# Banded attention and gated MLP on one core: folded score edges, a shared bank for the half middles, engine orders from a table, and a weight load in five pieces

## The chip, the cores and the metric

The kernel runs on one core of a Trainium2 chip (trn2). The metric is device time in microseconds (us) of one execution; lower is better. The core has five engines that each run their own instructions in order: PE (TensorE, matmuls), ACT (ScalarE), DVE (VectorE), POOL (GpSimd) and SP (SyncE, which here only issues DMAs). They wait for each other through semaphores.

## The reference

```python
mod = (_silu(c) @ w_mod).reshape(1, 6, 1, -1)          # sa, ca, ga, sb, cb, gb
h = _layernorm(x) * (1 + ca) + sa
x = x + ga * A(h, wqkv, wo)        # 16 heads of 28, S = 2048, D = 448
h = _layernorm(x) * (1 + cb) + sb
x = x + gb * B(h, w_in, w_sp, b_sp, w_out)

# A: causal attention in a window of 256 keys
mask = (i - j >= 0) & (i - j < 256)
p = softmax(where(mask, q @ k.T * Dh ** -0.5, -1e9));  o = (p @ v) @ wo
# B: gated MLP, Fh = 896
z = gelu(x @ w_in);  z1 = z[..., :Fh];  z2 = layernorm(z[..., Fh:])
g = w_sp @ z2 + b_sp               # w_sp is 2048 x 2048, over the tokens
out = (z1 * g) @ w_out
```

All tensors are bfloat16; the batch is 1.

## The kernel before

The 2048 tokens are 16 tiles of 128 (index j or t) and four blocks of 512 (tb). The 16 heads are four groups of four heads; a head takes 32 partitions, so that a group fills 128.

**Start.** Two x loads of two tiles each (`t_x0`, L427), `w_mod` (`t_wmA`) and the query and key weights (`t_wq`) are loaded on the DMA queues of SP and of ACT. DVE takes layernorm statistics of tiles 0 to 3 (L603), POOL the reciprocal root (L608, L609), DVE normalises (L616), PE transposes (L682) and ACT or DVE scale and shift into `hT` (L691, L693). `t_wqk` (L595, L596) casts the weights into `WQK`. PE then makes queries and keys (L760, L785) and values (L798).

**Attention.** A tile of queries needs key blocks j-2 (the old edge), j-1 (the middle, all 128 x 128) and j (the new edge, causal). It is worked in two halves of two head groups. For each half the score block (L901) writes four PSUM banks (0 to 3, one for each head of a group) with 36 small matmuls of 32 contraction rows: the middle of the first group (128 columns) and, for both groups, the old and the new edge folded together by 64 queries and keys into 192 columns. The middle of the second group comes from one matmul (L910) with `QBD`, a block-diagonal copy of the queries that four small DMAs fill from `qT` (L751, L777); it takes a fifth bank. ACT exponentiates (L862) 2048 columns of the four banks and 512 of the fifth, into a buffer of `PW`. DVE multiplies the folded edges by the mask into `PT` (L917, two for each half), and PE multiplies with the values (L944). DVE normalises the result into `o_sb` (L958, L960), a DMA transposes it, PE multiplies by `wo` (L969), DVE adds to x (L973), and the second layernorm follows (L603, L608, L609, L620, L616 or L622, a padding copy L625 or L626, a DMA transpose, L992 or L994).

**MLP.** PE multiplies by `w_in` in tiles of 64 rows: z2 (L1066) and z1 (L1087). ACT applies gelu (L1073, L1095), DVE normalises z2 (L603, L1078). SP issues 32 DMA transposes of `w_sp` into `wspA` and `wspB`, whose memory is that of `QBD`, `qT`, `KT` and `PT`, so that most of them wait for the end of attention. PE multiplies z2 by them (L1110, 28 groups of 16 matmuls), DVE adds `b_sp` (L1114), POOL multiplies by z1 (L1117), PE multiplies by `w_out` (L1127, 16 tiles), DVE adds x (L1137), and SP stores.

**Order.** Every operation is recorded with the engines it may run on, its dependences, a priority and a guessed duration. Before the program is written, `Sched.order` plays a greedy planner over these guesses: it fixes the order on every engine, the engine of each operation recorded by `either` or `free`, and the PSUM bank or buffer (`Hold`) each takes. `count` and `waits` then place semaphores. DMA landings of the first loads are given as fixed times (`land`). On the engines nothing is reordered.

Of the kernel before, what the change touches and what calls it, by code (L numbers as in the profile page):

```python
# [9 lines left out]
HOP = 0.12  # L10

BIAS = 0.0

NEXT = {"dve": 0.08, "act": 0.11, "pool": 0.045}

SHAPE = 0.1

TURN = 1.1
# [11 lines left out]
class Res:  # L30
# [6 lines left out]

    def best(self):
        found = None
        for o in self.options:  # L40
            at = 0.0
            for u in o:
                h = self.last[u]
                if h is None:
                    continue
                if not h.until or any(x.end is None for x in h.until):
                    at = None
                    break
                at = max([at] + [x.end for x in h.until])
            if at is not None and (found is None or at < found[0]):  # L50
                found = (at, o)
        return found
# [35 lines left out]
class Sched:  # L88
# [23 lines left out]
    def order(self):  # L112
        ready = {e: [] for e in ENGS}
        for op in self.ops:
            op.left = len(op.deps)
            for d in op.deps:
                d.users.append(op)
        free = {e: 0.0 for e in ENGS}
        table = [None]
        turned = [True]  # L120
        shape = ["full"]
        self.prog = {e: [] for e in ENGS}
        dma_at = [0.0]

        def enter(op):
            op.ready = max([0.0] + [d.start + d.ways["pe"][0] if d.eng == "pe" and "pe" in op.ways else d.end for d in op.deps])
            for e in op.ways:
                ready[e].append(op)

        for op in self.ops:  # L130
            if not op.left:
                enter(op)
        todo = len(self.ops)
        while todo:
            pick = None
            for e in ENGS:
                found = []
                for op in ready[e]:
                    if any(x.start is None for x in op.after):
                        continue  # L140
                    at = max(op.ready, free[e])
                    ok = True
                    for h in op.take:
                        b = h.res.best()
                        if b is None:
                            ok = False
                            break
                        at = max(at, b[0])
                    if ok:
                        found.append((at + (BIAS if e == "act" and len(op.ways) > 1 else 0.0), op))  # L150
                if not found:
                    continue
                first = max(free[e], min(a for a, _ in found))
                at, op = min(((a, o) for a, o in found if a <= first + 1e-9), key=lambda x: (x[1].prio, x[1].n))
                if pick is None or at < pick[0]:
                    pick = (at, e, op)
            assert pick is not None, "no op can go on"
            at, e, op = pick
            if e == "act" and len(op.ways) > 1:
                at -= BIAS  # L160
            for h in op.take:
                _, slot = h.res.best()
                h.slot = slot
                for u in slot:
# [5 lines left out]
            dur, fns = op.ways[e]  # L170
            if e == "act" and op.table and op.table != table[0]:
                dur += 1.3
            if e == "pe" and op.shape != shape[0]:
                dur += SHAPE
                shape[0] = op.shape
            if e == "sp":
                if op.turn and not turned[0]:
                    dur += TURN
                turned[0] = op.turn
            op.eng, op.start = e, at  # L180
            free[e] = at + dur - NEXT.get(e, 0.0)
            if op.land is not None:
                op.end = max(at + 1.0, op.land)
                dma_at[0] = max(dma_at[0], op.end - 2.0)
            elif op.dma:
                dma_at[0] = max(dma_at[0], at + 1.0) + op.lat
                op.end = dma_at[0] + op.tail
            else:
                op.end = at + dur + HOP + op.lat
            if e == "act" and op.table:  # L190
                table[0] = op.table
            for x in op.ways:
                ready[x].remove(op)
            self.prog[e].append(op)
            todo -= 1
            for u in op.users:
                u.left -= 1
                if not u.left:
                    enter(u)
# [1010 lines left out]
```

## Time and profile before

| | |
|---|---|
| timed runs | 289.79, 290.8, 291.15 us; median 290.8 |
| span of the profiled execution, first to last instruction | 288.0 us (the page gives no other time for it) |
| PE busy | 274.4 us (95%), 3432 matmuls |
| DVE, ACT, POOL busy | 170.3, 131.8, 123.4 us |
| DMA | 25.92 MB |
| granted PE clock | 1.00 throughout |

The page describes one execution; its durations are used against its own span of 288.0 us, which lies 2.8 us under the median of the timed runs. Differences worked out on the span are added to the median. "Busy" for PE counts pipelined matmuls to their modelled ends, so that two matmuls overlap in it: the distance from one start to the next says more of what a matmul costs than its duration does. A line of the form "A <- B: 5.6, 14, 0.5" says that A waited 5.6 us in total for B, 14 times, 0.5 us at most.

### The profile page before, as it was taken

To read this page: it belongs to the slowest core of one execution; us is meant where nothing else is said; L and a number is where in the kernel's file an instruction comes from. 1 tells how busy PE (TensorE), PEld (TensorE's weight loads), DVE (VectorE), ACT (ScalarE), POOL (GpSimd) and SP (SyncE) were. 2 spreads that over 40 slices of the span, in tenths; PEclk is the share of its full clock that TensorE was granted. 3 is DMA by queue.
4 is the path that set the end of the run, shared out by engine and by line. 5 is a ranking of instruction groups with operands and counts; after the bars stand their busy time and mean duration, and the time that the engine had idled before them with its cause. 6 is when DMAs were issued, how large, how long until landed. Compare 5 with 4: busy or idle time off the path is not lost.

```text
span 288.0 us, 7864 instructions
## 1 busy us (share of the span) xinstructions
PE 274.4 (95%) x3432; PEld 151.4 (53%) x3432; DVE 170.3 (59%) x365; ACT 131.8 (46%) x153; POOL 123.4 (43%) x192
## 2 busy tenths in 40 slices
PE   6798889999999999999979999999999999999997
PEld 2595557567666765544445544444444444444443
DVE  7679996988889999879998101113211231123223
ACT  4487979999999988775656720000000000000000
POOL 8041690761470749898654113333133303330331
DMA  7845936244233685320199899940100010001001
GB/s 213 267 156 148 326 60 95 54 83 92 39 41 76 112 166 58 60 58 18 39 186 167 194 175 190 186 77 17 49 0 0 2 64 0 2 0 64 0 2 64
DMA packets 65349, 25.92 MB, mean 90 GB/s; under 512 B 56417, under 2 KB 64226, under 8 KB 65314
## 3 DMA queue, kind: packets, MB, share of 16 engines
q1 hardware_dynamic: 64496, 24.26, 40.3%
q10 hardware_dynamic: 818, 1.15, 1.3%
q8 instruction: 27, 0.44, 0.7%
q14 instruction: 8, 0.07, 0.1%
HBM read 9.01 MB, written 1.84 MB: 38 GB/s over the span
## 4 chain that ended last, share of the span: by engine, by line
PE 64%; DVE 20%; POOL 5%; DMA 5%; issue 2%; SPq 2%; ACT 1%; ACTq 1%; POOLq 0%
PE ps L1110 34%; PE ps L1127 7%; PE ps L1087 5%; DVE st_all L603 5%; DVE PT L917 5%; PE ps L785 4%; DMA wq_st<-in_A_wqkv_dram 3%; PE ps L944 2%; POOL rs_all L609 2%; PE ps L798 2%; PE ps L1066 2%; PE ps L901 2%; PE ps L725 2%; DVE xn L616 1%; DVE x_sb L973 1%
## 5 line engine op out<-in xcount | busy, mean ns | idle before, releaser
L862 ACT ACTIVATE PW<-ps 128x2048 bf16<-128x2048 f32 (+1 forms) x56 | 69.4, 1239 | 4.5 <-PE ps L901 3.2
L1117 POOL TENSOR_TENSOR z1T<-tmpg,z1T 128x512 bf16<-128x512 bf16 x28 | 32.3, 1153 | 89.9 <-DVE tmpg L1114 89.9
L1114 DVE TENSOR_TENSOR tmpg<-ps,bsp_bc 128x512 bf16<-128x512 f32 x28 | 19.4, 692 | 85.3 <-PE ps L1110 85.3
L1110 PE MATMUL ps<-wspB,z 128*128 128x512 bf16 x224 | 48.8, 379 | 0.0
L1110 PE MATMUL ps<-wspA,z 128*128 128x512 bf16 x224 | 48.7, 379 | 0.0
L917 DVE TENSOR_TENSOR PT<-PW,mask 128x1024 bf16<-128x1024 bf16 x56 | 38.7, 718 | 0.7 <-ACT PW L862 0.3
L1110 PEld LDWEIGHTS ps<-wspA,z 128*128 128x128 bf16 x224 | 21.9, 98 | 26.5 <-issue 0.4
L1110 PEld LDWEIGHTS ps<-wspB,z 128*128 128x128 bf16 x224 | 21.9, 98 | 26.4
L608 POOL TENSOR_SCALAR ve_all<-mv_all 128x1 f32<-128x1 f32 (+2 forms) x37 | 10.1, 274 | 47.3 <-DVE mv_all L606 46.5
L944 PE MATMUL ps<-Vaug,PT 128*128 128x32 bf16 x496 | 26.2, 177 | 2.8 <-issue 1.7
L944 PEld LDWEIGHTS ps<-Vaug,PT 128*128 128x128 bf16 x496 | 22.9, 96 | 7.0 <-issue 1.8
L609 POOL TENSOR_TENSOR rs_all<-ve_all,neghalf 128x1 f32<-128x1 f32 (+2 forms) x37 | 24.8, 672 | 2.0
L1066 PE MATMUL ps<-w_in,hT 64*128 64x448 bf16 x224 | 22.4, 349 | 2.1 <-POOL rs_all L609 1.7
L1087 PE MATMUL ps<-hT,w_in 64*128 64x512 bf16 x196 | 21.8, 376 | 0.0
L1127 PE MATMUL ps<-w_out_g,z1T 128*128 128x448 bf16 x112 | 21.8, 352 | 0.0
L944 PE MATMUL ps<-Vaug,PW 128*128 128x32 bf16 x224 | 21.7, 176 | 0.0
L944 PEld LDWEIGHTS ps<-Vaug,PW 128*128 128x128 bf16 x224 | 17.9, 96 | 2.9
L603 DVE BATCH_NORM_STATS2 st_all<-x_sb 128x6 f32<-128x448 bf16 x32 | 18.9, 609 | 0.4 <-DMA x_sb<-in_A_x_dram 0.3
L1073 ACT ACTIVATE z<-ps 128x896 bf16<-128x896 f32 x16 | 13.9, 915 | 11.2 <-PE ps L1066 11.2
L603 DVE BATCH_NORM_STATS2 st_all<-z 128x6 f32<-128x448 bf16 x32 | 18.1, 594 | 1.0 <-ACT z L1073 1.0
L622 POOL TENSOR_SCALAR xn<-x_sb,rs_all,ve_all 128x448 bf16<-128x448 bf16 x17 | 18.1, 1066 | 0.9
L1066 PEld LDWEIGHTS ps<-w_in,hT 64*128 64x128 bf16 x224 | 11.0, 94 | 12.5 <-ACT z1T L1095 2.1
(106 smaller groups left out, 370.1 us busy)
## 6 DMA issues: line engine op xcount, KB each, us to landing
out_dram<-fin SPq DMA_DIRECT2D x16, 112.0 KB, 1.7
x_sb<-in_A_x_dram SPq DMA_DIRECT2D x3, 448.0 KB, 4.4
wmod<-in_w_mod_dram SPq DMA_DIRECT2D x1, 1344.0 KB, 8.0
w_in<-in_B_w_in_dram SPq DMA_DIRECT2D x1, 1344.0 KB, 8.2
w_out_g<-in_B_w_out_dram SPq DMA_DIRECT2D x1, 784.0 KB, 5.4
QBD<-qT SPq DMA_DIRECT2D x12, 64.0 KB, 2.0
bsp_bc<-in_B_b_sp_dram SPq DMA_DIRECT2D x1, 512.0 KB, 5.4
wmod<-in_w_mod_dram SPq DMA_DIRECT2D x2, 224.0 KB, 6.2
```

Of the source, the lines that this page charges most:

```text
L603: st = [dve(0.62 if True else 0, lambda e, t=t, ci=ci, s=s: e.bn_stats(st_all[:, slot, t, ci, :], s()), deps(t), prio) for ci, s in enumer ...
L609: rs = pool(0.53 + 0.15 * len(tiles), lambda e: e.tensor_tensor(rs_all[:, slot, a:b], ve_all[:, slot, a:b], neghalf[:, 0:b - a], ALU.pow), ...
L622: "pool": (0.9, lambda e: e.tensor_scalar(to[:, h.slot[0], 0:D], x_sb[:, t, :], z, ve, ALU.mult, ALU.add))}, [nm], prio, [h])
L862: ex = act(xdur, lambda e, out_ap=out_ap, in_ap=in_ap: e.activation(out_ap(), in_ap(), ACT.Exp, scale=SCALE), [s], v - 8.0 + u, takes, tab ...
L917: return dve(0.70, lambda e: e.tensor_tensor(cols(hp.slot[0] * 2048 + 1024 * k, [[256, 4], [128, 2], [1, 128]]), cols(at_w() + 128 + 192 * ...
L944: fns.append(lambda e, hp=hp, hO=hO, hi=hi, bi=bi, kb=kb, hd=hd, nb=nb, a=at[hi][bi], p_of=p_of: e.matmul(ps[:, hO.slot[0], 32 * hd:32 * h ...
L1066: return lambda e, kc, p0, start, stop: e.matmul(ps[:, hs[t % 2].slot[hf], 0:D], lhsT=hT[p0:p0 + 64, kc, t * 128:(t + 1) * 128], rhs=w_in[ ...
L1087: return lambda e, kc, p0, start, stop: e.matmul(ps[:, hs[b // 2].slot[b % 2], :], lhsT=w_in[p0:p0 + 64, kc, ft * 128:(ft + 1) * 128], rhs ...
L1110: m = pe(16 * MMS, [lambda e, h=h, si=si, ft=ft, tb=tb: e.matmul(ps[:, h.slot[0], :], lhsT=z2[:, si, ft * 128:(ft + 1) * 128], rhs=(wspA i ...
L1114: a = dve(0.7, lambda e, h=h, ht=ht, tb=tb: e.tensor_tensor(tmpg[:, ht.slot[0], :], ps[:, h.slot[0], :], bsp_bc[:, tb * 512:(tb + 1) * 512 ...
L1117: u = pool(1.16, lambda e, ht=ht, ft=ft, tb=tb: e.tensor_tensor(z1T[tb][:, ft, :], tmpg[:, ht.slot[0], :], z1T[tb][:, ft, :], ALU.mult), [ ...
L1127: return [lambda e, ft=ft: e.matmul(ps[:, h.slot[0], 0:D], lhsT=z1T[t // 4][:, ft, (t % 4) * 128:(t % 4 + 1) * 128], rhs=w_out_g[:, ft, :] ...
```

## The change

- **Edges folded by 32.** The old edge is computed for all 128 queries and the new edge written over its masked parts in pieces of 32 keys: 160 columns a group instead of 192, in 48 matmuls a half instead of 36. The mask reads `PW` with a step of 32 instead of 64.
- **Half middles.** The room gained in each bank (64 columns) takes 64 queries of the second group's middle. The other 64 queries of both halves come from two `QBD` matmuls of 256 columns into one bank, with one exponential of 512 columns for a tile instead of two. `QBD` is half as large, with runs of 128 elements in its DMAs (before 512 or 256), and zeroed by two instructions instead of four. `QP` reorders the groups in `qT`. `PW` has three buffers of a tile instead of five of a half.
- **Table.** The planner is replaced by `PLAN`: 1127 words, each an engine, an operation's number and its buffer choices. Some loads of the start change place: ACT's queue issues c, w_mod, the activation table load, w_q, and then the second x load, which was first. The 28 w_sp groups stand in another order, ahead of all `w_out` tiles.
- **w_in** is loaded in five pieces, each after a score block of tiles 4 to 8; before, three DMAs right after the x loads.
- Some guessed durations, landings and pacing dependences change.

```diff
+PLAN = """
+a0 d25 t32 s8 d27 t31 d26 a3 t33 s1 t35 t36 t34 d50 t37 p55.0 d24 s7 d23 p60.1 a42 d90 s5 t30 p57.2 d28 d91 s4
...
+p1018.4 d1117.3 s1122 s1118 p1123.7 d1019.2 s1020 p1124 d1125.1 s1126 p52.3
+"""
...
     def order(self):
-        ready = {e: [] for e in ENGS}
...
+        names = {"p": "pe", "a": "act", "d": "dve", "t": "pool", "s": "sp"}
         self.prog = {e: [] for e in ENGS}
...
+        for at, word in enumerate(PLAN.split()):
+            n, *slots = map(int, word[1:].split("."))
+            op = self.ops[n]
+            for h, k in zip(op.take, slots):
+                h.slot = h.res.options[k]
+                for u in h.slot:
                     old = h.res.last[u]
                     if old is not None:
                         op.deps.update(old.until)
                     h.res.last[u] = h
             op.deps.discard(op)
...
+            op.eng = names[word[0]]
+            assert op.eng in op.ways
+            op.end = at
+            self.prog[op.eng].append(op)
...
-    NPW = 5
+    NPW = 3
+    QP = (2, 0, 3, 1)
+    PWT = 576
+    PWH = 4 * PWT
...
-    QBD, _, qbd_bytes = alloc("QBD", [128, 2, 2, 4, 512], BF16, at=wspA_off)
+    QBD, _, qbd_bytes = alloc("QBD", [128, 2, 4, 2, 256], BF16, at=wspA_off)
...
-                 land=(3.0, 3.3)[i]) for i in range(2)]
+                 land=(3.65, 3.9)[i]) for i in range(2)]
...
-    t_win_l = load2("d_win", "sp", 1.4, w_in, ALL, B_w_in, ALL, prio=-46.0)
-
-    t_win_l.append(load("d_winc", "sp", 0.25, lambda e: e.dma_start(w_in[64:128, 3, :], B_w_in[384:448, :]), (), -45.9))
-    late += t_wo + t_win_l
+    late += t_wo
+    t_win_l = [load("d_win%d" % ch, "sp", 0.46, lambda e, ch=ch: e.dma_start(w_in[:, ch, :], B_w_in[ch * 128:(ch + 1) * 128, :]), (), -46.0 + 0.1 * ch)
+               for ch in range(3)]
+    t_win_l += [load("d_winh%d" % p0, "sp", 0.23, lambda e, p0=p0: e.dma_start(w_in[p0:p0 + 64, 3, :], B_w_in[384:448, :]), (), -45.6 + 0.001 * p0)
+                for p0 in (0, 64)]
...
-    PACE = {1: 0, 2: 18, 3: 34}
-    PSTEP = 1.0
+    PACE = {1: 0, 2: 15, 3: 27}
+    PSTEP = 0.75
...
-                        QBD[32 * hh:32 * hh + 32, tb % 2, :, hh, :],
-                        qT[32 * hh:32 * hh + 32, tb % 2].rearrange("p (a b) n -> p a b n", b=2)[:, :, 1, :]))},
+                        QBD[32 * hh:32 * hh + 32, tb % 2, hh].rearrange("p a (m n) -> p (a m) n", m=2),
+                        qT[32 * hh:32 * hh + 32, tb % 2, 0:2].rearrange("p a (m n) -> p (a m) n", m=2)[:, :, 64:192]))},
...
-                for place in (((0, m, 128, 0, 128, 0, 0),), ((k, o, 128, 0, 64, 128, 0) for k in range(2)), ((k, n, 128, 64, 128, 256, 0) for k in range(2)),
-                              ((k, *e) for k in range(2) for e in ((n, 64, 0, 64, 192, 0), (o + 64, 64, 64, 128, 192, 64)))):
...
+                places = [(0, m, 128, 0, 128, at_m0, 0)]
+                places += [(k, o, 128, 0, 128, at_f[k], 0) for k in range(2)]
+                places += [(1, m, 128, here, here + 64, at_hm, 0)]
+                places += [(k, n, 128, 96, 128, at_f[k] + 128, 0) for k in range(2)]
+                places += [(k, n + 32 * g, 32, 32 * g, 96, at_f[k] + 32 * (g + 1), 32 * g) for k in range(2) for g in range(3)]
...
-                unit(EPRI, MMS, [lambda e, hC=hC, m=m, half=half, qi=qs[1], j=j: e.matmul(
-                    ps[:, hC.slot[0], :].rearrange("p (h q) -> p h q", h=4), lhsT=KT[:, qi, m:m + 128],
-                    rhs=QBD[:, (j // 4) % 2, half, :, (j % 4) * 128:(j % 4 + 1) * 128], start=True, stop=True)],
-                     need + [q_dma[j // 4]], 0.6, to_e, lambda hC=hC: ps[:, hC.slot[0], :], [], hC)
...
+                    exC = unit(EPRI, 0.22, [lambda e, hC=hC, m=m, hh=hh, j=j, pair=pair: e.matmul(
+                        ps[:, hC.slot[0], 256 * hh:256 * hh + 256].rearrange("p (h q) -> p h q", h=4), lhsT=KT[:, 2 * hh + 1, m:m + 128],
+                        rhs=QBD[:, (j // 4) % 2, :, hh, pair:pair + 64], start=True, stop=True) for hh in range(2)],
+                         needC + [q_dma[j // 4]], 0.6, to_c, lambda hC=hC: ps[:, hC.slot[0], :].rearrange("p (a h q) -> p a h q", a=2, h=4), [], hC)
...
+    for n, d in enumerate(t_win_l):
+        d.deps.add(S_of[WIN_AT[n]][0])
```

More of the change, by code (lines that the diff above doesn't have):

```diff
@@ L36, in __init__ @@
         self.last = {u: None for u in units}
[L38 to L52, printed above, removed]
 class View(Res):
@@ L112, in order @@
     def order(self):
-        ready = {e: [] for e in ENGS}
[L114 to L121, printed above, removed]
-        self.prog = {e: [] for e in ENGS}
[L123 to L164, printed above, removed]
@@ L169, in order @@
             op.deps.discard(op)
[L170 to L199, printed above, removed]
+            op.eng = names[word[0]]
+            assert op.eng in op.ways
+            op.end = at
+            self.prog[op.eng].append(op)
+        assert sum(map(len, self.prog.values())) == len(self.ops)
     def count(self):
@@ L411, in load2 @@
         ]
-    t_c = load("d_c", "act", 0.01, lambda e: e.dma_start(c_row[:], c[0:1, :]), prio=-98.97, land=3.7)
+    t_c = load("d_c", "act", 0.01, lambda e: e.dma_start(c_row[:], c[0:1, :]), prio=-98.97, land=4.0)
     def x_load(e, i):
@@ L861, in unit @@
                 S_of[j].append(s)
-                ex = act(xdur, lambda e, out_ap=out_ap, in_ap=in_ap: e.activation(out_ap(), in_ap(), ACT.Exp, scale=SCALE), [s], v - 8.0 + u, takes, table="exp")
+                ex = act(xdur, lambda e, out_ap=out_ap, in_ap=in_ap: e.activation(out_ap(), in_ap(), ACT.Exp, scale=SCALE), [s] + list(after), v - 8.0 + u, takes, table="exp")
                 if exs:
```

144 lines of the change are left out of this document (103 added, 41 removed).

## The prediction

> **What bounds the kernel now.** I read the windows first, cut where the work changes: the first score block of tile 2 (30.1), the last product with the values (121.9), the first w_sp group (167.05), the last `w_out` matmul (285.1). Columns: stretch, length, then busy PE, PE weight loads, DVE, ACT, POOL with instructions.
>
> ```profile
> core 0: us, PE busy (x) PEld busy (x) DVE busy (x) ACT busy (x) POOL busy (x), PEclk, DMA share, GB/s
> 18.45:30.10 11.65, 10.10 (x175) 7.04 (x173) 9.69 (x24) 9.49 (x11) 4.12 (x8) 1.00 0.46 138
> 30.10:121.90 91.80, 87.81 (x2117) 58.02 (x2119) 83.56 (x171) 82.61 (x82) 53.78 (x82) 1.00 0.50 92
> 121.90:167.05 45.15, 43.01 (x415) 21.72 (x413) 34.51 (x85) 28.29 (x44) 26.37 (x55) 1.00 0.60 115
> 167.05:285.10 118.05, 118.05 (x563) 54.89 (x562) 28.52 (x43) 1.52 (x4) 32.30 (x28) 1.00 0.24 48
> ```
>
> After 167.05 PE never stops: only an earlier start of that stretch shortens the kernel. From 30.1 to 121.9 three engines are about 90% busy. Next the waits, which tell who holds whom there, and the groups with one shape a row.
>
> ```profile
> PEld ps L901 <- ACT PW L862: 5.6, 14, 0.5
> PE ps L901 <- ACT PW L862: 0.7, 2, 0.4
> ACT PW L862 <- PE ps L901: 3.2, 8, 0.6
> PE ps L910 <- DMA QBD<-qT: 1.1, 2, 0.7
> ```
>
> ```profile
> L862 ACT ACTIVATE PW<-ps 128x2048 bf16<-128x2048 f32 x28 | 52.7, 1881 | 3.7 <-PE ps L901 3.2
> L862 ACT ACTIVATE PW<-ps 128x512 bf16<-128x512 f32 x28 | 16.7, 598 | 0.8
> L917 DVE TENSOR_TENSOR PT<-PW,mask 128x1024 bf16<-128x1024 bf16 x56 | 38.7, 718 | 0.7 <-ACT PW L862 0.3
> ```
>
> The score block waits for its four banks, which the exponential of the half before still reads. Last the timeline, which gives distances between starts, the loads of the start and the w_sp transposes:
>
> ```profile
> 1.29 0.61 ACTq L413 DMA_DIRECT2D c_row<-in_c_dram  x1
> 1.93 0.40 ACTq L421 DMA_DIRECT2D wmod<-in_w_mod_dram  x1
> 2.36 0.49 ACTq L421 DMA_DIRECT2D wq_st<-in_A_wqkv_dram  x1
> 3.66 1.15 DVE L603 BATCH_NORM_STATS2 st_all<-x_sb 128x6 f32<-128x448 bf16 x2 [0.31 <-DMA x_sb<-in_A_x_dram]
> 12.99 1.06 PE L760 MATMUL ps<-hT,WQK 128*128 128x128 bf16 x16
> 142.63 20.20 SPq L479 DMA_TRANSPOSE wspA<-in_B_w_sp_dram  x14
> 167.05 3.19 PE L1110 MATMUL ps<-wspA,z 128*128 128x512 bf16 x14
> ```
>
> PE work from 30.1 to 121.9, by start distances: 28 score blocks 0.48 each, 27 `QBD` matmuls 0.22, 60 value products (12 matmuls in 0.295), 12 key blocks 0.895, 13 values and 14 `wo` tiles 0.765, 12 query blocks 0.86, 7 warming pairs 0.43, 1.5 of L1066: 83.0. So the 91.8 are 83.0 of work and 8.8 of waiting.
>
> **The change, part by part.**
>
> *Score block.* In one block of before, 4 matmuls of 128 columns take 0.05, 16 of 64 columns 0.10, then PE pauses about 0.1, 16 pieces of 64 keys run in 0.06 and it pauses 0.1 again: matmuls of different row groups run side by side, so columns count and not instructions. The new block has 0.05 + 0.107 (8 of 128) + 0.027 (4 of 64) + 0.027 (8 of 32), a pause, 24 pieces in two waves of 96 columns (0.08), a pause: 0.48 + 0.07 = 0.55. Bounds: 0.48 (all hidden in the pauses) and 48/36 x 0.48 = 0.64 (a fixed cost for each). x28: +2.0 (0 to +4.5).
>
> *Shared bank.* A `QBD` pair of 256 columns costs 0.22 once a tile, not twice: -3.1 of PE. ACT loses 14 x 0.598 = 8.4. The 2048-column exponential and the mask keep their sizes (steps of 576 and 32 elements instead of 512 and 64): nothing, bounds -/+0.03 on 56 masks. Zeroing `QBD` loses two instructions of 1.05 on ACT before 15 us, ahead of x: nothing.
>
> *What the table gives each engine,* from the order of instructions. ACT, first to last exponential: the 8.4, plus three key copies (0.597), two value copies (0.544), one query copy: -4.9 of 92. DVE, from the first `hT` to the last `o_sb`: three value copies, two key copies, three scalings (0.49), statistics of one tile less, two normalisations (0.503) and three paddings (0.309) more: -3.7. POOL -3.4, off the path.
>
> *Start.* The second x load is now last on ACT's queue. Before, that queue landed in order: x at 3.9 (224 KB), w_mod at 8.2 (448 KB more), w_q at 10.1 (448 more). The same bytes before it put x at about 10.1. DVE runs in order: its statistics of tiles 2 and 3 stand ahead of the casts of `WQK` and the copies to `modT`, and PE's first queries wait for these. 10.1 + two statistics 1.07 + aggregate 0.1 + two xn 0.7 + aggregate 0.15 + POOL's add and power 1.47 (6.21 to 7.68 before) + two xn 0.7 + two casts 0.69 + `hT` 0.4 + hops 0.3 = 15.6, against 12.99: +2.6 (low end +0.7, if it lands with w_mod at 8.2). The first exponential goes with it, 20.46 to 23.0. ACT has the last query copy behind that, so it ends at 24.6 (before 21.2, on DVE). The `QBD` DMAs on SP wait for it, behind them the x loads of blocks 2 and 3 (+3.4); PE's first `QBD` matmul waits for the DMAs: 25.6 + 3.4 = 29.0. The table puts it ahead of tile 2's score block: 29.2, where before it was 30.1. The late start is thus not lost twice, but paid in work moved behind: half of tile 1's scores, two values, one key block.
>
> *Attention.* PE's work behind 29.2 is 83.0 - 3.1 + 2.0 + 3.2 (moved) = 85.1. The waits: a half of a tile has 0.175 less of ACT (4.9/28) and 0.13 less of DVE (3.7/28); 0.15 x 28 = 4.2 off PE's 8.8, most of which were for exponentials. Bounds: 0 (the order ties PE elsewhere) and 6.8 (2 us left). Waits 4.6.
>
> *w_in.* SP waits for PE (tiles 4 to 8) before each piece, and block 1's fourth `QBD` copy stands behind the first, as do four transposes of xn. A 448 KB load took 4.4 to land, so that copy lands some 5.4 after the score block of tile 4; the `QBD` matmul is due 4.6 after it: up to 0.8, I take +0.4. The DMAs of 26 to 36 us get room, worth nothing, as x did not wait for them after 28.2.
>
> The `QBD` copies move half the bytes in runs of 256 B (before 1 KB). Landing took 2.0 for 64 KB in 1 KB runs and 2.1 for 32 KB in 512 B runs: a fixed time, so nothing. [...]
>
> *Tail.* From the last `o_sb` (122.4) to the first w_sp group were 44.7. PE has 42.0 of work there; the table puts 22 us of it, not 11, ahead of what needs block 2, which ends the wait of 1.7 at 145.9. But the last `hT` transpose came 18.9 after that `o_sb`, behind it 14 transposes of w_sp at 1.44, the last landing 3.8 after its issue: 42.9. Now it is 15 (one of `wspB` has slipped in) and DVE has 0.3 more ahead: 44.5. So 44.7 stays. `b_sp` is loaded after 29 transposes instead of before `wspB`: about 69.9 after the last `o_sb`; the ninth group needs a free bank at 72.3. Hidden, with 2.4 to spare; what is later than that PE waits. Group and `w_out` order: 28 x 3.45 + 16 x 1.33, as before.
>
> Sum: 29.2 + 85.1 + 4.6 + 0.4 = 119.3 against 121.9: -2.6, so a span of 285.4, and 290.8 - 2.6 = **288.2**.
>
> **Rivals.**
> *Waits that grow (slower).* The table was fixed for guessed times, with the second x load at 3.9; an order that meets another timing makes each engine stand before the wrong instruction. In PE's attention, waits a third over 8.8 (11.7) give 29.2 + 85.1 + 11.7 + 0.4 = 126.4, +4.5: 295.3; waits of 8.7 already give +1.5, the point from which it is slower. For it: three engines at 90%, and DVE blocked on x to 10.1. Against: ACT and DVE are lighter.
> *w_sp takes the gain (no difference).* If DVE's z2 statistics, five of which stand ahead of the last tiles' additions, push the last `hT` transpose 2 later, the groups start 2 later whatever attention gained: 290.2.
> *x lands early or order gains more.* Queues that interleave would land x near 5; or the order leaves 2 of waiting. Either is worth 2.6 more: 285.6. Against: the queue's order at 3.9, 8.2, 10.1.
> That the table does not do what it says is excluded by the listed order.
>
> **How the numbers follow.** Runs of this kernel tell apart about 0.5% (1.45 us): the three lie within 1.36. Forecast 0.42, x early or better order 0.15, both faster: 0.57. w_sp: 0.18, within 0.5%. Waits that grow: 0.25. The range goes from 282.5 (order and x both, 5.7 below) to 294.0 (two thirds of the slower case's price) and leaves out the far part of that case and little below. The faster cases alone: 282.5 to 289.3.
>
> **What would show it.** First L760 matmul near 15.6, and DVE's third statistics waiting for x to about 10; ACT's 128x512 exponentials 14 instead of 28; score blocks at 0.55; PE's waits for `PW` about half; the last `o_sb` near 119.8, first w_sp group 44.7 later. Wrong, if the first queries start at 13, if PE waits over 8.7 in attention, or if the group start moves without the `o_sb`.

## The result

The changed kernel takes **294.26 us** (median of four runs, 293.11 to 295.28); the kernel before took 290.3 us (289.05 to 291.15). The ratio is 1.0135, 95% interval 1.0104 to 1.0166. It is slower by 1.35%; the forecast was 288.2, from 282.5 to 294.0.

| point, us from the start of the span | before | forecast | changed |
|---|---|---|---|
| first query matmul (L760, now L733) | 12.99 | 15.6 | 15.46 |
| first exponential (L862, now L839) | 20.46 | 23.0 | 22.79 |
| tile 2's first score block (L901, now L883) | 30.1 | 29.2 | 28.9 |
| last product with the values ends (L944, now L930) | 121.9 | 119.3 | 126.0 |
| last `o_sb` (L960, now L946) | 122.39 | 119.8 | 126.33 |
| first w_sp group (L1110, now L1099) | 167.05 | 164.5 | 170.49 |
| end of the span | 288.0 | 285.4 | 291.4 |

All that was lost against the forecast was lost between the third and the fourth row.

### The profile page after: what moved, and what is told of

It is laid out like the page before. It is cut to its first block, busy times and chain, and to the rows that moved or that the text cites. A ratio compares the mean times of both kernels' runs of the same rounds, so it can differ in the third digit from the quotient of the medians.

```text
span 291.4 us, 8478 instructions
## 1 busy us (share of the span) xinstructions
PE 275.1 (94%) x3768; PEld 153.9 (53%) x3768; DVE 164.5 (56%) x361; ACT 126.1 (43%) x147; POOL 116.7 (40%) x186
## 4 chain that ended last, share of the span: by engine, by line
PE 68%; SPq 9%; ACT 8%; DMA 6%; DVE 4%; POOL 3%; issue 1%; ACTq 0%
PE ps L1099 33%; SPq L452 7%; PE ps L1116 7%; ACT PW L839 5%; PE ps L883 5%; PE ps L930 5%; PE ps L771 3%; PE ps L698 3%; PE ps L955 3%; PE ps L758 3%; DMA QBD<-qT 2%; DMA x_sb<-in_A_x_dram 2%; PE ps L544 2%; PE ps L1055 2%; PE ps L894 1%
## 5 line engine op out<-in xcount | busy, mean ns | idle before, releaser
L839 ACT ACTIVATE PW<-ps 128x2048 bf16<-128x2048 f32 (+1 forms) x42 | 60.2, 1451 | 12.0 <-PE ps L883 9.0
L1103 DVE TENSOR_TENSOR tmpg<-ps,bsp_bc 128x512 bf16<-128x512 f32 x28 | 18.6, 688 | 81.6 <-PE ps L1099 52.9
L1099 PE MATMUL ps<-wspA,z 128*128 128x512 bf16 x224 | 49.3, 379 | 2.4 <-DMA wspA<-in_B_w_sp_dram 2.4
L1099 PE MATMUL ps<-wspB,z 128*128 128x512 bf16 x224 | 49.2, 379 | 0.0
L902 DVE TENSOR_TENSOR PT<-PW,mask 128x1024 bf16<-128x1024 bf16 x56 | 37.8, 700 | 3.7 <-ACT PW L839 3.7
L1099 PEld LDWEIGHTS ps<-wspA,z 128*128 128x128 bf16 x224 | 21.9, 98 | 29.0 <-issue 2.9
L1099 PEld LDWEIGHTS ps<-wspB,z 128*128 128x128 bf16 x224 | 21.9, 98 | 26.4
L930 PE MATMUL ps<-Vaug,PT 128*128 128x32 bf16 x496 | 24.1, 177 | 1.2 <-DVE PT L923 1.1
L582 POOL TENSOR_TENSOR rs_all<-ve_all,neghalf 128x1 f32<-128x1 f32 (+2 forms) x37 | 23.6, 642 | 1.7
L930 PEld LDWEIGHTS ps<-Vaug,PT 128*128 128x128 bf16 x496 | 21.8, 96 | 4.4 <-DVE PT L923 1.2
L930 PE MATMUL ps<-Vaug,PW 128*128 128x32 bf16 x224 | 20.3, 176 | 0.0
L883 PE MATMUL ps<-qT,KT 32*128 32x128 bf16 (+5 forms) x1344 | 17.6, 199 | 1.4 <-ACT PW L839 1.2
L930 PEld LDWEIGHTS ps<-Vaug,PW 128*128 128x128 bf16 x224 | 17.7, 96 | 1.4 <-issue 0.2
L883 PEld LDWEIGHTS ps<-qT,KT 32*128 32x128 bf16 (+1 forms) x1344 | 13.7, 91 | 8.8 <-ACT PW L839 4.7
L1084 ACT ACTIVATE z1T<-ps 128x512 bf16<-128x512 f32 x28 | 14.7, 604 | 7.3 <-PE ps L1076 7.3
```

The source lines that it names most:

```text
L582: rs = pool(0.53 + 0.15 * len(tiles), lambda e: e.tensor_tensor(rs_all[:, slot, a:b], ve_all[:, slot, a:b], neghalf[:, 0:b - a], ALU.pow), ...
L839: ex = act(xdur, lambda e, out_ap=out_ap, in_ap=in_ap: e.activation(out_ap(), in_ap(), ACT.Exp, scale=SCALE), [s] + list(after), v - 8.0 + ...
L883: fm.append(lambda e, hm=hm, qi=qi, key=key, kn=kn, lo=lo, hi=hi, col=col, p0=p0, t=t, j=j: e.matmul(ps[p0:p0 + kn, hm.slot[t], col:col + ...
L902: return dve(0.70, lambda e: e.tensor_tensor(cols(hp.slot[0] * 2048 + 1024 * k, [[256, 4], [128, 2], [1, 128]]), cols(at_w() + pad + at_f[ ...
L930: fns.append(lambda e, hp=hp, hO=hO, hi=hi, bi=bi, kb=kb, hd=hd, nb=nb, a=at[hi][bi], p_of=p_of: e.matmul(ps[:, hO.slot[0], 32 * hd:32 * h ...
L1099: m = pe(16 * MMS, [lambda e, h=h, si=si, ft=ft, tb=tb: e.matmul(ps[:, h.slot[0], :], lhsT=z2[:, si, ft * 128:(ft + 1) * 128], rhs=(wspA i ...
```

## The profile after

The windows answer, cut at the same events of the changed kernel (columns as before):

```profile
core 0: us, PE busy (x) PEld busy (x) DVE busy (x) ACT busy (x) POOL busy (x), PEclk, DMA share, GB/s
28.95:126.00 97.05, 91.61 (x2500) 63.38 (x2502) 82.23 (x173) 79.38 (x77) 46.86 (x73) 0.98 0.52 97
126.00:170.49 44.49, 42.09 (x408) 19.85 (x408) 35.68 (x89) 29.95 (x46) 28.06 (x58) 1.00 0.67 118
170.49:288.55 118.06, 118.06 (x561) 54.91 (x562) 27.52 (x43) 0.04 (x1) 31.76 (x28) 1.00 0.25 50
```

Attention has grown from 91.8 to 97.05 although ACT's work in it fell from 82.6 to 79.4. ACT's idle time went from 9.2 to 17.7: its work is 3.2 less and the stretch 5.25 longer. (ACT lost 14 x 0.598 = 8.4 us of exponentials, but makes more key and value copies there, 8 instead of 5 and 11 instead of 9.) The last stretch is what it was. And PEclk is 0.98 in attention: part of it ran at less than the full clock.

ACT's groups in that stretch, one shape a row, and the waits of the whole execution:

```profile
L839 ACT ACTIVATE PW<-ps 128x2048 bf16<-128x2048 f32 x28 | 52.6, 1878 | 9.9 <-PE ps L883 9.0
L839 ACT ACTIVATE PW<-ps 128x512 bf16<-128x512 f32 x14 | 8.4, 597 | 2.1 <-PE ps L894 1.9
```

```profile
ACT PW L839 <- PE ps L883: 9.0, 16, 2.0
...
PEld ps L883 <- ACT PW L839: 4.7, 10, 1.3
...
PE ps L894 <- DMA QBD<-qT: 2.8, 3, 1.8
...
PE ps L1099 <- DMA wspA<-in_B_w_sp_dram: 2.4, 1, 2.4
```

The exponentials are 14 fewer at the same price each, as forecast. But ACT now waits 9.0 for score blocks, where it waited 3.2. The last two lines are waits for DMAs: for the `QBD` copies and, before the first w_sp group, for w_sp.

The row PEld (4.7, before 5.6) is not what PE lost: it is idle time of the weight loads, which overlap the matmuls (both start at 105.14 in the rows below). PE's own row for the same wait was 0.7 in two pieces before (the prediction shows it below the 5.6) and is 1.2 here, also in two. Three rows of the kernel before show the difference, then PE's own row of the changed one:

```profile
105.14 0.44 PEld L901 LDWEIGHTS ps<-qT,KT 32*128 32x128 bf16 x36 [0.37 <-ACT PW L862]
105.14 0.55 PE L901 MATMUL ps<-qT,KT 32*128 32x128 bf16 x36
107.73 0.55 PE L901 MATMUL ps<-qT,KT 32*128 32x128 bf16 x36 [0.37 <-ACT PW L862]
```

```profile
PE ps L883 <- ACT PW L839: 1.2, 2, 0.8
```

The 2048-column exponential ahead of the block at 105.14 ended at 104.76, and the block started 0.28 behind the start of the last matmul before it. At 48.65 the exponential had ended 1.0 earlier (47.64), and the block started at the same 0.28, its weight loads idle for the same 0.37. Of the 14 waits in the PEld row of before 12 are of this kind: the exponential had been over for 0.17 to 1.02 us. Only at 107.73 and 113.34 did the block start 0.06 behind the exponential's end, and PE lost about 0.4 each time.

Around the longest wait for `QBD`, the chain of waits and then the windows, each 3.41 us long like the two stretches of this execution with a granted clock of 0.50 (12.02 to 15.43 and 104.18 to 107.59):

```profile
99.32 0.70 DVE PT L902
100.02 0.17 SPq L452
100.19 0.04 issue
100.24 0.60 SPq L724
...
102.17 1.89 DMA QBD<-qT
104.06 0.05 issue
104.10 0.57 PE ps L894 x2
```

```profile
97.36:100.77 3.41, 3.41 (x107) 2.84 (x106) 3.04 (x7) 2.67 (x4) 0.00 (x0) 1.00 1.11 113
100.77:104.18 3.41, 1.61 (x20) 0.84 (x18) 3.29 (x8) 2.05 (x2) 0.80 (x2) 1.00 0.47 105
104.18:107.59 3.41, 3.41 (x70) 1.99 (x71) 0.61 (x2) 2.47 (x2) 0.00 (x0) 0.50 0.65 78
```

Block 3's last query copy ends at 97.45, but its four `QBD` copies stand on SP behind two w_sp transposes and one of hT, are issued from 100.24, and the last lands at 104.06; PE stands before tile 12's `QBD` matmuls for 2.0 us. In that window of 3.41 us PE is busy for 1.61; in the next one the granted clock is 0.50, and some 1.4 us are lost to longer matmuls: from start to start the `QBD` pair takes 0.50 instead of 0.22, the score block 0.82 instead of 0.55, the four `wo` matmuls 1.47 instead of 0.81 (at 101.03), and the matmuls behind them 0.2 more. The same happens at the start (PE busy 1.68 of 3.41 from 8.61, clock 0.50 from 12.02).

Executions of one kernel differ in how many such windows they have, so each is counted here from its span and mean granted clock (0.988 over 291.4 us are two). The changed kernel had 2, 2, 3 and 3; the kernel before, over some hundred runs beside the experiments, about 1.0 in the mean. Least squares over the runs of every kernel, with one price for a window, gives 1.28 us a window (95% within 0.14; runs with more than four windows or 2% above their kernel's median are left out), and without any window 289.4 us for the kernel before and 291.0 for the changed one. So of the 4.0 us, 1.5 windows more account for 1.9, and some 1.6 are there without them (only four runs stand behind the changed kernel's figure: 95% within 0.8). "Without windows" below means this figure.

## The experiments

Theory A: the fixed order makes PE stand before late operands, and half clock follows. Theory B: the new arithmetic itself does not shorten attention. Theory C: the late x load made the kernel slower.

**The order of the first loads.** First only ACT's x load moved up, then all of them as in the kernel before:

```diff
-a0 ... a3 ... a42 ... a6 d89 a2
+a0 ... a2 a3 ... a42 ... a6 d89          (x_first)
-... s8 ... s1 ... s7 ... s5 ... s4       SP: w_q, x, w_q, w_mod, w_mod
+... s1 s4 s5 s7 s8                       (start_order; on ACT a2 a0 a3 a42 a6)
```

> The changed kernel with the second x load issued second on ACT's queue (behind c, ahead of w_mod and w_q) instead of last; everything else of the table is kept. Theory A (fixed order that stands before late operands, and the half clock that follows such waits): the first query matmul moves from 15.4 to about 13, tile 2's first score block from 28.9 to about 26.5, but the waits behind it are mostly unchanged in kind; the kernel gains what it starts earlier, 2 to 2.6 us, to about 292. Theory B (the new arithmetic itself is dearer: more PE work and an exponential that nothing covers while the score block is made): the same start, the same 97 us of attention, about 292. Theory C (the late load alone made the kernel slower than before): it comes down to before's time or under it, 288 to 290.

295.09 us (ratio to before 1.0121, 1.0072 to 1.0169). The first query matmul did not move (16.05): the first matmul with w_mod, which now stands behind x on ACT's queue, came at 10.4 instead of 8.7, and SP's own x load still stood second, behind a piece of the query weights.

> The changed kernel with the issues of the first loads in the order of the kernel before on both queues: x first on SP and on ACT, then w_mod, then the query and key weights; the rest of the table is kept. The earlier run with only ACT's x load moved did not start earlier, since SP's x load still stood behind a piece of the weights and w_mod came later. Theory A and C (the late start is what the table loses): first query matmul at about 13.3 instead of 15.4, everything behind it 2 us earlier, about 292 with the half clocks of the changed kernel, 288.5 for an execution without any. Theory B (the attention is bound by itself): the same 2 us, since nothing catches up a late start. If the order of the loads is not the reason, the first query matmul stays at 15 and the time at 294.

292.31 us (1.0038, 1.0008 to 1.0068). The first query matmul comes at 12.72, tile 2's score block at 26.45, attention ends at 121.92. The 2.5 us of the start arrive undiminished behind attention: nothing catches up a late start, and nothing had been catching it up. But little of it reaches the end: the last `o_sb` is 3.9 earlier than in the changed kernel, the first w_sp group 2.8 (PE waits 3.6 for w_sp instead of 2.4, and a half clock follows at 168.45), the end of the span 1.1. Without windows this kernel stands at 291.3, the changed one at 291.0; its better median goes with fewer windows (1.25 a run in the mean against 2.5). The run also ends theory C as the whole answer: without the late load the kernel is still not faster than before. Its attention takes 95.5 us at full clock:

```profile
26.45:121.92 95.47, 90.17 (x2499) 62.89 (x2498) 81.72 (x172) 79.08 (x77) 46.59 (x73) 1.00 0.57 98
```

**The order in attention.** The waits for `QBD` taken away on SP, and the table replaced by the planner of before:

```diff
-... s760 s759 ... s464 ... s284 s287 s285 s286     (w_sp, w_sp, hT, four QBD copies)
+... s284 s287 s285 s286 s464 ... s760 s759          (q_early; also s232 ahead of s21)
```

> The changed kernel with three SP entries moved: block 3's four QBD copies ahead of two w_sp transposes and a transpose of the normalised x, and block 2's fourth copy ahead of the w_in piece. Theory A: the waits of 2.0 and 0.7 us before the QBD matmuls of tiles 12 and 8 go, and with the first the half clock that followed it (104.2 to 107.6, 1.5 us of longer matmuls): attention ends 3 to 4 us earlier, about 290.5. Theory B: the score block of the next tile then waits for its exponential instead; gain under 1 us, about 293.5. If the half clock stays although the wait is gone, it is not the wait that brings it.

293.98 us (1.0108, 1.0070 to 1.0145). The waits for `QBD` are gone from the list of waits and no window of attention is at half clock, but attention still takes 94.8 us: PE now stands 1.1 us among tile 14's products with the values and 0.5 behind tile 13's second score block, where it did not before. Without windows the runs stand at 290.5, 0.5 below the changed kernel. That is theory B's figure, but not its place: the new waits are not at a score block.

> The changed arithmetic (edges folded by 32, half middles in one bank, w_in in five pieces) with the planner of before in place of the table. Theory A (the table's order is what costs): attention takes about 90 us, the kernel 286 to 289, faster than before. Theory B (the arithmetic costs): attention stays at 95 us or more and the kernel at 293 or more. The second x load is then early again, which by itself is worth up to 2.6 us and must be taken off before the two are compared.

295.09 us (1.0132, 1.0089 to 1.0176; `Sched.order` and `Res.best` of before, the first pair of w_in groups confined to banks 0 to 3). Theory A expected 286 to 289 and falls as the main cause: the other order is no better although the second x load is early again, 291.1 without windows, with 97.7 us from tile 2's score block to the last product, two half-clock windows among them.

**Parts of the change alone, in the kernel before.** First what the shared bank takes away, at an unchanged order:

```diff
+                nq = 8 if half else 128
...
-                    ps[:, hC.slot[0], :].rearrange("p (h q) -> p h q", h=4), lhsT=KT[:, qi, m:m + 128],
-                    rhs=QBD[:, (j // 4) % 2, half, :, (j % 4) * 128:(j % 4 + 1) * 128], ...
+                    ps[:, hC.slot[0], 0:4 * nq].rearrange("p (h q) -> p h q", h=4), lhsT=KT[:, qi, m:m + 128],
+                    rhs=QBD[:, (j // 4) % 2, half, :, (j % 4) * 128:(j % 4) * 128 + nq], ...
```

> The kernel before, same order, with the second half's QBD matmul and its exponential narrowed from 512 columns to 32 (what it leaves out: the middle of the second half's second group, in whose place the first group's probabilities are used). This takes from before what the shared bank takes: ACT 14 x 0.4 = 5.6, PE 14 x 0.2 = 2.8, at an unchanged order. The prediction's reasoning (waits follow the work of ACT): the waits fall with it, 284 to 287. Theory B (that exponential ran while PE made the next score block, which needs it not; nobody waits for it, and the fixed order hands the time on to nobody): at most PE's 2.8 and more likely under 1.5, 289 to 290.

290.89 us (0.9993, 0.9962 to 1.0023); without windows 288.0, 1.4 below the kernel before. Waits and ACT's groups in its attention:

```profile
PEld ps L901 <- ACT PW L862: 5.7, 14, 0.7
PE ps L901 <- ACT PW L862: 0.9, 2, 0.6
```

```profile
L862 ACT ACTIVATE PW<-ps 128x512 bf16<-128x512 f32 x14 | 8.4, 597 | 0.3
L862 ACT ACTIVATE PW<-ps 128x32 bf16<-128x32 f32 x14 | 2.8, 198 | 0.4
```

ACT has 5.6 us less to do, and neither row fell: 5.7 for the weight loads (before 5.6), 0.9 for PE itself (before 0.7). What frees the four banks is the 2048-column exponential; the short one came behind it, while PE made the next block, and nobody stood for it. PE's own `QBD` matmuls are some 2.6 shorter here (14 x 0.19 between starts), so even of PE's work only about half is gained.

Then the fold, with a shorter exponential:

```diff
-                for place in (((0, m, 128, 0, 128, 0, 0),), ...
+                places = [(0, m, 128, 0, 128, 0, 0)]
+                places += [(k, o, 128, 0, 128, 128 + 160 * k, 0) for k in range(2)]
+                places += [(k, n, 128, 96, 128, 256 + 160 * k, 0) for k in range(2)]
+                places += [(k, n + 32 * g, 32, 32 * g, 96, 160 + 160 * k + 32 * g, 32 * g) for k in range(2) for g in range(3)]
...
-                to_a = lambda at_w=at_w: PW[:, at_w():at_w() + 2048]
+                to_a = lambda at_w=at_w, cols=cols: cols(at_w(), [[512, 4], [1, 448]], PW)
```

> The kernel before, same order, with only the edges folded by 32: 48 matmuls in a score block instead of 36, and its exponential over 448 columns of a bank instead of 512 (nothing is put into the freed room, the QBD matmuls and their exponentials stay). The score block becomes 0.54 instead of 0.48, the exponential about 1.67 instead of 1.88. Theory B (the chain score block, exponential, score block sets the attention): 28 x (0.21 - 0.06) = 4.2 less, 286. The prediction's accounting (PE's work sets it, waits follow ACT): +1.7 for the block and some waits less, 288 to 291. If the order hands nothing on: 290 to 292.

292.92 us (1.0082, 1.0057 to 1.0108), 290.2 without windows, 0.8 above before. ACT's row:

```profile
L862 ACT ACTIVATE PW<-ps 128x1792 bf16<-128x1792 f32 x28 | 46.6, 1664 | 10.5 <-PE ps L903 9.7
```

Each exponential is 0.217 shorter, 6.1 us in all, and ACT's wait for score blocks went from 3.2 to 9.7, 6.5 more; 2.6 of it is one stop of PE inside a score block at 35.3, for which the profile names no engine and behind which a half clock came (38.70). Theory B as it was written here, a chain of block and exponential that sets the time, falls too: a link of that chain became shorter and the kernel longer. What remains fits both runs: PE hardly stood for exponentials, so time given back on ACT becomes idle time on ACT, and a dearer block is paid (28 x 0.06 = 1.7 of work; the 0.8 has a 95% interval of 0.8 to either side).

Last the late pieces of w_in, put into the kernel before, and taken out of the changed one (on top of the reordered loads):

```diff
-    t_win_l = load2("d_win", "sp", 1.4, w_in, ALL, B_w_in, ALL, prio=-46.0)
+    t_win_l = [load("d_win%d" % ch, ...) for ch in range(3)] + [...]     (win5)
+    for n, d in enumerate(t_win_l):
+        d.deps.add(S_of[WIN_AT[n]][0])
```

```diff
-... s16 ... s17 ... s18 ... s19 ... s20 ... s21 ... s22
+... s16 ... s17 s18 s19 s20 s21 s22                                      (win_back; no wait for score blocks)
```

> The kernel before with w_in alone in five pieces, each behind a score block of tiles 4 to 8; its planner orders the rest anew. Theory A and the prediction's step (the loads of w_in are hidden in both places, a QBD copy behind a piece costs up to 0.4): 290.6. Theory D (the DMA room that is free at 26 to 36 us lets block 1 start earlier): 288 to 289. If the planner's order takes it badly: 292 or more.

> The changed kernel with the first loads reordered (292.31 us), and with the five pieces of w_in issued where before had w_in, right behind the loads of wo at about 27 us, without waiting for score blocks. The pieces alone, put into the kernel before, took it to 294.55. If the late pieces cost by themselves (they stand ahead of QBD copies and transposes on SP and share the DMA engines with them): 290 to 291, the QBD waits at tiles 8 and 12 shorter. If it was the planner's new order that took them badly, and the table placed them well: 292.3 or more, since the transposes of o_sb behind them at 28 us then share the DMA engines with 1.6 MB.

win5 took 294.55 us (1.0139, 1.0091 to 1.0187), win_back 294.0 (1.0098, 1.0065 to 1.0131). In the kernel before the pieces cost 3 us beyond windows, but its planner moved other work with them, so how much is the pieces' own stays open. Taken out of the changed kernel they change nothing beyond windows (291.0 against 291.3; the median is 1.7 higher, with 2.2 windows a run instead of 1.25): they are not where its gain went.

**The half clock.** Warming matmuls in a wait: in the wait for tile 12's `QBD` (four pairs), and before the first w_sp group, on top of the reordered loads (six pairs):

```diff
+    for _ in range(4):                    # range(6) and bG in the tail
+        hW = Hold(bC)
+        hW.until.append(pe(0.46, [lambda e, hW=hW: e.matmul(
+            ps[:, hW.slot[0], :].rearrange("p (a b) -> p a b", b=128), lhsT=ident[:], ...) for _ in range(2)], [t_ident], 900.0, [hW]))
-... p629.0
+... p1127.0 p1128.0 p1129.0 p1130.0 p629.0
```

> The changed kernel with four pairs of warming matmuls (into the bank of the shared middles) right before the QBD matmuls of tile 12, where PE waited 2.0 us for the QBD copies: the wait for the copies stays, PE is busy in it. Theory A (a 3.4 us window in which PE is busy less than about half is followed by 3.4 us at half clock): the attention's half clock at 104 goes, longer matmuls worth 1.5 us go with it; about one window less per execution, 292.7. Rival (the half clock comes from something else, power or the stall's DMA): it stays, 294.3.

295.49 us (1.0138, 1.0097 to 1.0178). Attention had no half clock in the profile, but the start had two such windows and the tail one, and the runs with moved loads had none in attention either, without such pairs and with waits of 1.0 and 1.6 us there. It tells nothing.

> The changed kernel with the first loads reordered (its run took 292.31 us, with a half clock from 168.4 right behind PE's wait of 3.6 us for wspA), and with six pairs of warming matmuls between the last w_in matmul and the first w_sp group: PE waits for wspA as long as before, but is busy for about 2.6 of the 3.6 us. Theory A (half a window without matmuls brings 3.4 us at half clock): the half clock at 168 goes and the kernel gains about the 2 us by which executions with one such window differ from those without, 290.2 in the median. Rival (the half clock answers to something else at that place, such as the start of the w_sp groups): unchanged, 292.3, or later by the warming matmuls.

293.92 us (1.0105, 1.0056 to 1.0155). The pairs were put into banks that gelu was still reading: PE stood 2.5 us, the half clock came at 166.2, and the pairs ran in it for 4.2 us and pushed the first group to 170.91. A mistake of placing.

> As the run with warming matmuls ahead of the first w_sp group, but in the two banks that the first two groups take next and that are read out first; in the run before, the warming pairs stood 2.5 us for a bank that gelu still read, ran at half clock behind that and held the groups up by 3.2 us. Theory A (a window that is half idle brings the half clock): PE is busy at once, no half clock at 166 to 171, 290 to 291 in the median against 292.31 without the pairs. Rival: it comes all the same, 292 or more. If the pairs stand for a bank again, the run says nothing.

In the profile PE goes from the last w_in matmul to the pairs without a stop and the whole execution has the full clock; the first group starts at 167.50, as late as without the pairs, and the span is 288.4 against 290.3. The windows without the pairs, and the same stretch with them:

```profile
165.04:168.45 3.41, 0.71 (x4) 0.38 (x5) 0.00 (x0) 1.58 (x4) 0.00 (x0) 1.00 1.11 192
168.45:171.86 3.41, 3.41 (x10) 1.22 (x9) 0.00 (x0) 0.00 (x0) 0.00 (x0) 0.50 0.93 179
```

```profile
164.20:167.50 3.30, 3.22 (x19) 1.15 (x16) 0.00 (x0) 2.96 (x6) 0.00 (x0) 1.00 0.91 180
```

The timed runs do not confirm it: 293.19 us (1.0085, 1.0054 to 1.0116), with windows in 9 of 12 runs, about as many as without the pairs (8 of 9). Only the profiled one shows where its windows lie, so whether the others were at the start stays open. Without windows it stands at 291.3, as without the pairs.

**The transposes of w_sp.** The halved `QBD` leaves half of wspA's memory free from the start, and the table still loads only two of its sixteen blocks early. Six more at 31 us; four more in the kernel before, which has a quarter free; then five more in two places, with the reordered loads, and also with the `QBD` copies moved:

```diff
-        deps = [S_of[11], q_dma[2]] if si in (0, 1, 2, 3, 8, 9) else [all_S, list(q_dma.values())]
+        deps = [] if si >= 8 else ...                  (early_w; in the two last [t_x[1]]; in before: [t_x[3]] if si >= 12)
-... s319 ...                                           ... s767 to s772 in the tail
+... s319 s767 s768 s769 s770 s771 s772 ...             (early_w)
+... s767 s768 s139 ... s319 s769 s770 s771 ...         (best_a0, best_a)
```

> The changed kernel with six of the sixteen wspA transposes issued at about 31 us on SP, into the part of wspA's memory that the halved QBD leaves free, instead of behind the last transpose of normalised x. Theory A: PE's wait of 2.4 us for wspA before the first w_sp group goes, and with it a half clock of 3.4 us that falls behind it in some executions (1.7 us): 290 to 292. Theory B: the same 2.4 us. Rival: the transposes hold up the loads of x, wo and the transposes of o_sb behind them and attention ends that much later: 294 or more.

292.42 us (1.0070, 1.0043 to 1.0098). The first group starts 41.9 behind the last `o_sb` instead of 44.2, but the six transposes take 10.55 us on SP instead of 8, and block 1's `QBD` copies come late; PE stands 2.5 us before them and a window at half clock follows.

> The kernel before with four more wspA transposes issued early, into the quarter of wspA's memory that is free in it; PE's order is unchanged. If the chain of SP transposes sets the first w_sp group of before (167.05), it starts up to 2.5 us earlier and the kernel takes 288 to 289. If PE's own work and its wait at 146 set it, no change: 290.4.

295.23 us (1.0144, 1.0094 to 1.0194). Slower than before, with PE's order untouched:

```profile
29.38 0.63 SPq L448 DMA_DIRECT2D w_in<-in_B_w_in_dram  x1
30.05 1.36 SPq L479 DMA_TRANSPOSE hT<-o_sb  x1
31.46 8.46 SPq L479 DMA_TRANSPOSE wspA<-in_B_w_sp_dram  x3
39.97 2.12 SPq L479 DMA_TRANSPOSE hT<-o_sb  x1
```

Right behind the loads of w_in a transpose of w_sp takes 2.8 us; in the tail it was 1.44. What stands behind them, transposes of `o_sb` and the `QBD` copies, is late, and two windows at half clock follow at 48.5.

> The changed kernel with the first loads issued in the order of before, and with five more wspA transposes issued early on SP (two behind the second x load at about 17 us, three behind the first transpose of o_sb), into the memory that the halved QBD leaves free. The run with six of them in one place held up block 1's QBD copies by 2.3 us and gained in the tail what it lost there. Theory A: the first w_sp group starts about 42.5 us behind the last o_sb instead of 45.3 and is not followed by a half clock: start at about 165, 287.5 to 288.5, below the kernel before. Theory B says nothing against it: attention as in the run with the reordered loads (95.5 us). Rival: the transposes hold up other loads again, 290 or more.

> The same, and with block 3's QBD copies ahead of two w_sp transposes and block 2's last one ahead of the w_in piece. Theory A (waits for QBD are what the table loses): 2 us less than the run without this, since PE then waits neither 1.6 us at tile 12 nor 0.5 us at tile 9. Theory B (the waits only move to the next exponential): within 0.7 us of it.

best_a0 took 289.34 us (0.9944, 0.9908 to 0.9979); best_a **288.36 us (0.9919, 0.9886 to 0.9952)**, faster than both kernels. Its windows, in an execution at full clock (span 284.9):

```profile
26.90:121.83 94.93, 90.09 (x2499) 62.99 (x2498) 81.76 (x171) 78.94 (x76) 46.49 (x73) 1.00 0.60 107
121.83:164.02 42.19, 42.19 (x413) 19.96 (x409) 35.66 (x89) 27.48 (x42) 28.06 (x58) 1.00 0.63 111
```

Attention is still 94.9. From the first query matmul (12.86) to the last product are 109.0 us, against 108.9 before. The whole gain is the tail: PE has no idle time left in it, 42.19 us instead of 45.15, and w_sp, which ended it before, is ready. In this run the change pays there, by memory that it frees, and not in attention, which it was made in. That the change is needed for it is not shown: the kernel before has four blocks of wspA free, and no run loads them at these two places of the start (in the run above they stood behind w_in). Here the moved `QBD` copies were worth 1.0 in the medians (289.34 to 288.36; in the changed kernel 294.26 to 293.98).

## Why the prediction was wrong

**The start** was right: 15.6, 23.0, 29.2 forecast, 15.46, 22.79, 28.9 measured, as the queue's order had it. Its closeness is in part luck: the x load landed at 9.58 instead of 10.1, and warming matmuls at half clock (four in 1.91 us), which the forecast did not have, stood between the transposes.

**PE's work** was right: score blocks 0.54 (0.55), `QBD` pairs 0.22, and 97.1 us less the waits give 85.1 behind tile 2's block, as forecast. (Three slips weigh little: the list of PE's work in the kernel before adds up to 83.3, not 83.0; the parts named for a score block add 0.08, not 0.07, and 0.06 came; order and x together are worth 5.2, not 5.7, at the low end of the range.) The `QBD` copies, in 256 B runs now, landed in 2.0 at the median (twelve of 32 KB; four of 16 KB in 2.3), against 2.0 and 2.1 before.

**The waits** were wrong, and with them the sign. The failing step reads "0.15 x 28 = 4.2 off PE's 8.8, most of which were for exponentials". By the distances between starts PE waited 12.0 instead of 4.6 + 0.4: 3.4 in 34 small handovers of about 0.1, about 1.4 of half clock, 2.7 for `QBD` (0.4 were allowed for the copy behind the w_in piece; the copies of block 3, behind w_sp on SP, were not seen), 1.2 for a mask of tile 1, 1.0 ahead of tile 15, the rest in waits of 0.2 to 0.6. Against the kernel before, attention has 2.2 more of work and 3.1 more of waits.

The premise is what failed. The 8.8 are hardly waits for exponentials: the row that suggests it, 5.6 in 14, is the weight loads', and PE's own row beside it says 0.7 in two. By the distances between starts 3.0 of the 8.8 are 30 handovers of about 0.1, most of them at a score block, whether its exponential was long over or not; 1.9 is one stop at 35 for which no engine is named; only two blocks stood for exponentials, with 0.8 to 1.0 in all. PE's rows of this stretch name ACT or DVE for 1.7 in all, exponentials included, so 4.2 was not there to be had from lighter engines. half_c and fold_same bear this out: they took 5.6 and 6.1 us off ACT at a fixed order, and the one gained 1.4 without windows (with 2.6 less of PE's own work), the other nothing. Even in the execution of best_a, at full clock and with no wait for `QBD` behind tile 2's first block, PE waited some 10 around 85 of work. Which of these waits the order makes and which any order would have stays open.

**The moved work** was booked as a late start "paid in work moved behind", and the gain was to come on top. start_order shows the late start passed on in full to the end of attention.

**The tail** was right as a distance: 44.2 from the last `o_sb` to the first group (44.5 to 44.7), set by SP's transposes, PE waiting 2.4 for them; b_sp hidden (PE busy through 118.06). That the freed half of wspA's memory could end this wait was missed.

**The rival** "waits that grow" gave 126.4 for the end of attention and 295.3 for the kernel; 126.0 and 294.26 came. Its size was right, and its point of decision (waits of 8.7), but its reason only in part: PE did stand before late `QBD` copies, but the planner's order does no better with this arithmetic. Nothing in the forecast had the half clock, which accounts for some 1.9 of the 4.0 us.

## What to carry to other kernels

Before a named wait is counted as something to gain, look whether the busy engine itself stood: take its own row and the distances between its starts, not the row of its weight loads, and look when the named instruction ended. Where it had ended earlier, shortening it moves idle time to its engine and gains nothing (in fold_same ACT had 6.1 us less of work and 6.5 more of waits). Before an order is rewritten, look at what each in-order queue has ahead of a small copy that the busiest engine waits for. Look for the gain of freed memory in the loads that could not start before.

## What the runs showed of the hardware

In the changed kernel's execution the granted clock is 0.50 in the 3.41 us from 12.02 and from 104.18. These two starts lie 92.16 us apart, 27 times 3.413. Cut at that step, windows of this execution, and of two experiments at their own half clock, show:

| run | window, us | PE busy, us | granted clock in the next window |
|---|---|---|---|
| start_order | 165.04 to 168.45 | 0.71 | 0.50 |
| early_w | 46.90 to 50.32 | 1.33 | 0.50 |
| changed | 100.77 to 104.18 | 1.61 | 0.50 |
| changed | 8.61 to 12.02 | 1.68 | 0.50 |
| changed | 169.02 to 172.43 | 1.94 | 1.00 |
| changed | 5.20 to 8.61 | 2.11 | 1.00 |
| changed | 35.91 to 39.32 | 2.28 | 1.00 |

These rows do not show where between 1.68 and 1.94 the difference begins, nor whether PE's busy time alone makes it. The wait of 2.0 us ahead of tile 12 fell into one window (1.61 busy), and half clock followed; the 2.4 us ahead of the w_sp group at 170.49 fell across two (2.49 and 1.94 busy), and the clock stayed at 1.00. The kernel before had a wait of 1.87 us at 35 and kept its clock; where its windows lie is not shown, since its profiled execution has no half clock. So a wait of some 2 us may cost 1.3 us more than itself (an estimate, from the 1.28 us a window above), depending on where the windows lie in that execution.
